# Weights spread over partitions through DRAM, V transposed by DMA, another beginning: one change to a four-layer attention kernel

## The chip, the cores and the metric

The program runs on one core of one Trainium2 chip. The metric is the device time of one execution in microseconds (us). Engines: PE (TensorE), ACT (ScalarE), DVE (VectorE), POOL (GpSimd) and SP (SyncE, which here only issues DMAs); PE's weight loads are listed apart as PEld.

## The reference

x has 2048 rows of 1024 values; there are 32 heads of width 32. Two kinds of layer alternate, each behind a layer norm and each added to x:

```python
def _A_ref(x, wqkv, w_phi, wo):                 # linear attention
    q, k, v = split_heads(x @ wqkv)
    pq = einsum("bhsd,hdf->bhsf", q, w_phi);  pk = einsum("bhsd,hdf->bhsf", k, w_phi)
    phi_q = concatenate([softmax(pq), softmax(-pq)], -1)
    phi_k = concatenate([softmax(pk), softmax(-pk)], -1)
    kv = einsum("bhsf,bhsd->bhfd", phi_k, v);  z = einsum("bhsf->bhf", phi_k)
    num = einsum("bhqf,bhfd->bhqd", phi_q, kv)
    den = einsum("bhqf,bhf->bhq", phi_q, z)[..., None] + 1e-6
    return merge_heads(num / den) @ wo

def _B_ref(x, wqkv, wo):                        # softmax attention
    q, k, v = split_heads(x @ wqkv)
    p = softmax(einsum("bhqd,bhkd->bhqk", q, k) * Dh ** -0.5)
    return merge_heads(einsum("bhqk,bhkd->bhqd", p, v)) @ wo

x = A_x
for _ in range(2):
    x = x + _A_ref(_layernorm(x), A_wqkv, A_w_phi, A_wo)
    x = x + _B_ref(_layernorm(x), B_wqkv, B_wo)
```

## The kernel before, in words

**Layout.** x lies transposed in SBUF for the whole run (`xT`: 1024 features as 8 tiles of 128 partitions, 2048 rows as four *chunks* of 512). A projection of one 128-feature tile for one chunk is eight groups of four matmuls: `mm` splits each 128-wide weight tile into four of 32 columns (rows of the profile with `128*32 128x512`, L529; four such run beside each other on four parts of the array). PSUM has eight banks of 128x512.

**Order.** Nothing is issued where it stands in the source. Each instruction is handed to a list scheduler (`op`, `dma`) with an engine, a planned duration, its dependences, its buffers and a due time (`prio`); the scheduler simulates the engines and buffers and so fixes one order for every engine beforehand. On the chip each engine, and each DMA-issuing queue (SP, ACT and POOL have one each), goes through its list strictly in order and waits where an input isn't there. The tables at the head of the file (`COUNT`, `KP`, `VQ`, `OUT`, ...) are due times and choices for this planner.

**Layer A.** Keys first: features of K, then `kv` and `z` sums over all rows. Then queries, chunk by chunk (c = 0..3), each in two halves of 16 heads (hf = 0, 1), by `a_queries`: four projected 128x512 tiles; ACT takes exp(+) and exp(-) of each; matmuls with `rep` (L938) sum them per head; ACT takes Ln of both sums, DVE subtracts (L948), ACT takes Exp: a *weight* for every head and row, 4 heads in 4 rows of each of four 32-row bands. To multiply it in, it has to be spread over the 32 partitions of its head. `split_hl` (DVE: L891, L892) splits the f32 weight into two bf16 parts, `spread` (PE, L907, stationary operand `selb`) copies it over partitions into PSUM banks, and DVE multiplies exp(-) by it (L955, four per half). Numerators (L970) and denominators (L985) follow; the denominator's reciprocal (ACT: Ln, Exp) is spread in the same way, but *turned* by a band for each tile (`selr`), and DVE multiplies the numerators by it (L996). `a_out` projects the result, and DVE adds it to `xT` (L1009). Then the next layer norm of that chunk starts.

**Layer B.** For each query chunk and each of eight groups of four heads: score matmuls (L1231), exponentials, matmuls with V and with ones (L1279). Most exponentials are ACT's (L1247, on 1536 or 1024 columns at a time); `COUNT` says, for each of 32 (chunk, group) pairs, how many pairs of 512-column units are left to DVE, which computes them by integer arithmetic (`pair`: L1158 twice, L1167, L1170, L1172, L1175, L1177). The sums' reciprocals are written to DRAM (`rd`, L1336) and read back over 32 partitions each (L1338), for DVE's multiplication at L1344. K, Q and V for later groups, weights of layer A and so on are fitted between as *fill* (buffer class "fil"). Keys go to their place by DMAs (L1025), swapped queries by L1046/L1047. PE also issues matmuls without use (`idle`) when it would fall idle. V is computed with the chunk's rows stationary, 256 columns at a time (`b_v`; evacuated by ACT at L1032 or by DVE at L1033).

**Beginning.** Chunk 0 of x is brought in by eight transposing DMAs (L561), SP's and ACT's queue by turns. Layer A's K weights are folded with w_phi (`fold_phi`): their first half is loaded by POOL's queue, their second by SP's (L711), then PE transposes them (L724). Later weights come as slabs (L684, L687). `phi_t` is a constant tile that DVE clears.

Of the kernel before, what the change touches and what calls it, by code (L numbers as in the profile page):

```python
# [12 lines left out]
ALU = mybir.AluOpType  # L13
# [36 lines left out]
LAT = {"PE": 0.2, "ACT": 0.19, "DVE": 0.06, "POOL": 0.2, "SP": 2.0, "AQ": 2.0, "GQ": 2.5}  # L50
# [5 lines left out]
TIE = 9  # L56
# [13 lines left out]
class Sched:  # L70
# [99 lines left out]
    def run(self):  # L170
# [32 lines left out]
        while left:  # L203
# [108 lines left out]
SBUF_ARENA = 172 * 1024 - 256  # L312
# [3 lines left out]
LONG = {"kT", "v", "slab", "slabk", "xn", "xn1", "kvacc", "kvm", "zm", "wnat"}  # L316
MODEST = {"slabk", "xn1", "e1", "vp1", "pkf", "lnw1", "w2o"}
NUMS = 2
LATER = ((33.8, 20.9, 28.9, 13.4), (31.9, 22.9, 4.6, -2.5))
VQ = (((0, 7.0), (45.5, 3.6), (55.2, 7.3)), ((10.4, 7.5), (84.2, 12.8), (150.7, 10.1)))  # L320
FULL = 5
OUT = (37.1, 25.3)
EARLY = (4.0, 0.0)
DUE = 0.0
BOOST = 30.0
EVAC = 20.0
QA = (101.9, 4.8)
# [4 lines left out]
         "rs": 8, "pkf": 1, "cden": 2, "part": 8, "w2r": 1,  # L332
# [8 lines left out]
HOST = ((), (16,), (11, 17), (5, 11, 22), (5, 10, 18, 24))  # L341
# [3 lines left out]
SLABD = (1, 5)  # L345
TOK = (0.0, 0.6, 0.61, 0.62)
SLOW = 6.0
HALF = 4
KGAP = (6.2, 2.4)
LATE = 15.8  # L350
KP = (0, 40.9, 68.0, 103.5, 68.1, 148.3, 180.6, 204.5)
BO = 225
OP0 = (233.8, 267.8, 288.4)
OGAP = (2.5, 2.1, 1.7)
COUNT = ((0, 0, 0, 2, 4, 4, 4, 3, 4, 3, 4, 4, 4, 4, 4, 3, 4, 2, 3, 4, 3, 2, 1, 2, 0, 2, 4, 2, 1, 2, 3, 4),
    (2, 4, 4, 4, 4, 4, 3, 4, 4, 4, 4, 4, 4, 4, 4, 4, 4, 4, 4, 4, 4, 4, 5, 4, 4, 2, 4, 4, 4, 3, 4, 2))
PAIRS = ((), ((0, 2),), ((0, 2), (1, 2)), ((0, 1), (0, 5), (1, 3)), ((0, 1), (0, 5), (1, 1), (1, 5)),
    ((0, 1), (0, 3), (0, 6), (1, 1), (1, 5)), ((0, 1), (0, 3), (0, 6), (1, 1), (1, 3), (1, 6)))
AK = ((0, 201.9), (1, 232.4), (2, 258.8))
OUT1 = ((171.2, 2.7), (179.5, 1.3), (245.9, 1.0))  # L360
# [14 lines left out]
def kernel(  # L375
# [52 lines left out]
    phi_t = const.tile([P, G * P], BF16, tag="phi")  # L428
    nc.vector.memset(phi_t[:].bitcast(U32), 0)
# [24 lines left out]
    for a in range(4):  # L454
        for j in range(4):
            c = (j + a) % 4
            nc.vector.tensor_copy(
                out=selr[32 * a:32 * a + 32, 32 * c:32 * c + 32], in_=selb[32 * a:32 * a + 32, 32 * j:32 * j + 32])
# [16 lines left out]
    gone = []  # L475
    qd = dram_p.tile([P, 2 * G * C512], BF16, tag="qd")
# [78 lines left out]
    def load_x():  # L555
        for lo, hi, prio, us, kb in ((0, 1, -24.0, 1.3, 128), (1, 2, -9.0, 1.3, 400), (2, NC, -8.0, 2.0, 800)):
            last = []
            for po in range(PO):
                q = "AQ" if not lo and po % 2 else "SP"
                last.append(dma(  # L560
                    prio, lambda lo=lo, hi=hi, po=po, q=q: ENG[q].dma_start_transpose(  # L561
                        out=xT[:, po, lo * C512:hi * C512], in_=A_x[0, lo * C512:hi * C512, po * P:(po + 1) * P]),
                    q=q, issue=us, kb=kb))
                if not lo:
                    last[-1].slack = 1.2
            for c in range(lo, hi):
                xdone[c] = last
# [134 lines left out]
    def phi():  # L702
        return phi_t[:].rearrange("p (g n) -> p g n", g=G)

    def fold_phi(col, wd_v, prio, use_pe):
        w_t = []
        if use_pe:
            nb, nv = sb("wnat", PO, D)
            ld = []
            for h, q, at in ((0, "GQ", -23.0), (1, "SP", -20.0)):  # L710
                ld.append([dma(at, lambda h=h, i=i, q=q: ENG[q].dma_start(  # L711
                    out=nv()[:, 2 * i:2 * i + 2, C512 * h:C512 * h + C512],
                    in_=A_w[:, 2 * i:2 * i + 2, col + C512 * h:col + C512 * h + C512]),
                    (), [nb], q=q, kb=256, issue=0.7) for i in range(4)])
                for o in ld[-1]:
                    o.slack = 1.2
# [25 lines left out]
        for fc in range(2):  # L742
# [3 lines left out]
            for m in range(PO):  # L746
                pb, pv = ps("wt", ANY)

                def fn(m=m, pv=pv, fc=fc):
                    for k in range(4):  # L750
# [3 lines left out]
                       [pb] + [w_t[4 * fc + k][0] for k in range(4)], pa, mode="c")  # L754
# [157 lines left out]

# [652 lines left out]
```

## Time and profile before

| | |
|---|---|
| time, median of 3 runs | 2269.91 us (2265.57 to 2270.1) |
| the profiled execution | 2261.7 us; its span 2259.7 us |
| granted PE clock | 1.00 |
| busy: PE, ACT, DVE, POOL | 2170.3, 1987.8, 1844.7, 197.2 us |
| first layer A ("A1") | 0 to 337.0 us |
| first layer B ("B1") | 337.0 to 1222.3 us |
| second layer A ("A2") | 1222.3 to 1424.9 us |
| second layer B ("B2") | 1424.9 to 2248.6 us, then 11.1 us of output |

The borders are the first and the last start of an L1247 exponential in each layer B. A phase of layer A includes the layer norm and the first projections for the layer B behind it. PE's busy time in the phases of layer B includes the matmuls without use, so there a high share does not say that PE is the bound.

### The profile page before, as it was taken

The page shows a single profiled execution, that of the slowest core. Times are in us where ns is not written, and L with a number is a line of the kernel's source. Part 1 is how long each engine was busy: PE and PEld are TensorE (multiplying, and loading weights), DVE is VectorE, ACT ScalarE, POOL GpSimd, SP SyncE. Part 2 cuts the span into 40 slices and gives each one's busy share as a digit, 9 for nine tenths or more (in the row PEclk, how much of TensorE's full clock was granted, in tenths as well). Part 3 has the DMA queues.
Part 4 walks back from the last instruction along what each step waited for, and adds up shares of the span by engine and source line. Part 5 has one row for each costly group of instructions (what it writes and reads, how often), then busy time and mean ns, then how long its engine had stood idle before and what let it go on. Part 6 is the DMA issues. An engine that isn't in the chain of part 4 may idle for free.

```text
span 2259.7 us, 82520 instructions
## 1 busy us (share of the span) xinstructions
PE 2170.3 (96%) x36752; PEld 869.3 (38%) x36752; DVE 1844.7 (82%) x2754; ACT 1987.8 (88%) x1939; POOL 197.2 (9%) x301
## 2 busy tenths in 40 slices
PE   5999999999999999999999999999999999999999
PEld 3554454344333333333333444433333333333333
DVE  6887772498899779678788788799899999997986
ACT  4435759999999999999998555899999999999998
POOL 1020000000001010121224100000000000100000
PEclk9999999999999999999999999999999999999999
DMA  8320011111123231222235101111111101201111
GB/s 180 68 67 23 9 42 40 45 33 26 45 62 108 63 82 40 68 82 82 82 109 152 40 5 30 33 28 34 39 32 28 40 19 26 72 24 42 47 35 38
DMA packets 123085, 119.67 MB, mean 53 GB/s; under 512 B 59944, under 2 KB 100968, under 8 KB 122728
## 3 DMA queue, kind: packets, MB, share of 16 engines
q1 hardware_dynamic: 102392, 56.64, 9.8%
q0 software_dynamic: 17584, 56.70, 8.8%
q8 instruction: 287, 4.70, 0.9%
q10 hardware_dynamic: 2752, 1.05, 0.2%
q14 instruction: 70, 0.57, 0.1%
HBM read 78.71 MB, written 14.14 MB: 41 GB/s over the span
## 4 chain that ended last, share of the span: by engine, by line
PE 29%; ACT 20%; DVE 10%; issue 6%; DMA 1%; POOL 0%; SPq 0%; ACTq 0%; DVEq 0%; POOLq 0%
ACT arena L1247 19%; PE psum L529 15%; PE psum L1279 6%; PE psum L1231 6%; DVE arena L1177 1%; DVE arena L1158 1%; DVE arena L1175 1%; DVE arena L1170 1%; DVE arena L1167 1%; DVE arena L1344 1%; DVE arena L1172 1%; ACT arena L799 1%; DMA arena<-arena 1%; DVE arena L1033 0%; DVE arena L1295 0%
## 5 line engine op out<-in xcount | busy, mean ns | idle before, releaser
L1247 ACT ACTIVATE arena<-psum 128x1536 bf16<-128x1536 f32 (+1 forms) x1366 | 1671.2, 1432 | 10.7 <-PE psum L1231 6.0
L529 PE MATMUL psum<-arena 128*32 128x512 bf16 (+1 forms) x18432 | 1055.2, 357 | 15.4 <-issue 3.9
L529 PEld LDWEIGHTS <-arena 128*32 128x32 bf16 x18944 | 461.1, 96 | 445.3 <-issue 171.7
L1279 PE MATMUL psum<-arena 128*32 128x512 bf16 x4096 | 624.4, 383 | 4.5 <-DVE arena L1295 3.5
L1279 PE MATMUL psum<-arena,ones_bf 128*32 128x512 bf16 x4096 | 624.1, 383 | 1.3 <-issue 1.3
L1231 PE MATMUL psum<-arena 32*128 32x512 bf16 x4096 | 537.1, 383 | 32.9 <-ACT arena L1247 25.9
L1231 PEld LDWEIGHTS <-arena 32*128 32x128 bf16 x4096 | 157.3, 91 | 561.3 <-issue 554.6
L1158 DVE TENSOR_SCALAR arena<-psum 128x512 int32<-128x512 f32 x414 | 280.8, 684 | 102.8 <-PE psum L1231 96.4
L1177 DVE SCALAR_TENSOR_TENSOR arena<-arena 128x1024 int16<-128x1024 int32 x207 | 251.5, 1216 | 4.2 <-PE psum L1279 0.2
L1279 PEld LDWEIGHTS <-arena 128*32 128x32 bf16 x4096 | 163.5, 95 | 225.4 <-issue 174.7
L1279 PEld LDWEIGHTS <-ones_bf 128*32 128x32 bf16 x4096 | 161.2, 95 | 25.3 <-issue 10.2
L1167 DVE TENSOR_SCALAR arena<-arena 128x1024 f16<-128x1024 int16 x207 | 141.2, 686 | 5.3 <-DMA arena<-arena 1.6
L1170 DVE TENSOR_TENSOR arena<-arena 128x1024 f16<-128x1024 f16 x207 | 140.7, 683 | 5.3 <-DMA arena<-arena 0.6
L1175 DVE TENSOR_TENSOR arena<-arena 128x1024 f16<-128x1024 f16 x207 | 140.8, 683 | 3.4
L684 POOL DMA_DIRECT2D arena<-in_B_wqkv_dram x46 | 42.1, 915 | 1095.4 <-PE psum L529 320.9
L1033 DVE CAST arena<-psum 128x512 bf16<-128x512 f32 x128 | 87.4, 683 | 59.6 <-PE psum L529 59.4
L799 ACT ACTIVATE arena<-psum 128x512 bf16<-128x512 f32 x80 | 43.1, 596 | 83.5 <-PE psum L529 60.6
L803 DVE TENSOR_REDUCE arena<-arena 128x32 f32<-128x1024 bf16 x64 | 77.2, 1213 | 36.8 <-ACT arena L799 36.6
L529 PE MATMUL psum<-xT,onesD 128*32 128x512 bf16 x1112 | 99.5, 381 | 1.1 <-DVE arena L1033 0.5
L1295 DVE COPY arena<-psum 128x512 f32<-128x512 f32 x126 | 86.1, 683 | 14.2 <-PE psum L1279 13.9
L812 DVE TENSOR_TENSOR arena<-psum,arena 128x1024 bf16<-128x1024 f32 x64 | 77.5, 1218 | 13.3 <-PE psum L529 9.8
L1172 DVE TENSOR_SCALAR arena<-arena 128x1024 f16<-128x1024 f16 x207 | 86.4, 421 | 1.9
(120 smaller groups left out, 1378.9 us busy)
## 6 DMA issues: line engine op xcount, KB each, us to landing
arena<-rd SPq DMA_DIRECT2D x62, 256.0 KB
arena<-in_B_wqkv_dram POOLq DMA_DIRECT2D x58, 256.0 KB, 4.2
arena<-in_B_wo_dram POOLq DMA_DIRECT2D x40, 256.0 KB, 4.0
arena<-in_A_wqkv_dram POOLq DMA_DIRECT2D x36, 256.0 KB, 4.8
arena<-arena SPq DMA_DIRECT2D x256, 32.0 KB
arena<-wd_k POOLq DMA_DIRECT2D x32, 256.0 KB, 4.7
arena<-arena SPq DMA_DIRECT2D x96, 64.0 KB
arena<-arena SPq DMA_DIRECT2D x248, 2.0 KB
```

Source lines behind the costliest of these rows:

```text
L529: nc.tensor.matmul(out_[ks, :], lhsT=lhsT[:, ks], rhs=rhs, start=start, stop=stop, tile_position=(0, 32 * k), skip_group_check=True)
L1033: return op("DVE", dve_us(512), lambda: nc.vector.tensor_copy(out=dst(), in_=src()), [dep], bufs, prio)
L1158: o = op("DVE", dve_us(512), lambda: nc.vector.tensor_scalar(out=x_v()[:, k, :].bitcast(I32), in0=s_v()[:, x * C512:(x + 1) * C512], scala ...
L1167: last = op("DVE", 1024 / 1920 + 0.15, lambda: nc.vector.tensor_scalar(out=z(), in0=x_v().bitcast(I16).rearrange("p a (n two) -> p a n two ...
L1170: last = op("DVE", 1024 / 1920 + 0.15, lambda: nc.vector.tensor_tensor(out=u(), in0=z(), in1=z(), op=ALU.mult), [last], [z_b, u_b], prio + ...
L1172: last = op("DVE", 1024 / 3840 + 0.15, lambda: nc.vector.tensor_scalar(out=u(), in0=u(), scalar1=POW2_C[0], scalar2=POW2_C[1], op0=ALU.mul ...
L1175: last = op("DVE", 1024 / 1920 + 0.15, lambda: nc.vector.tensor_tensor(out=u(), in0=z(), in1=u(), op=ALU.mult), [last], [z_b, u_b], prio + ...
L1177: return op("DVE", dve_us(1024), lambda: nc.vector.scalar_tensor_tensor(out=y_v().bitcast(I16), in0=x_v().bitcast(I32), scalar=128.0 / BIT ...
L1231: nc.tensor.matmul(out=s_v()[:, x * C512:(x + 1) * C512], lhsT=kT[g][1]()[r, pp, d * P:(d + 1) * P], rhs=q_of[(qc, g)][1]()[r, (pp + j // ...
L1247: ex = op("ACT", act_us(w * C512), lambda s_v=s_v, e_v=e_v, w=w: nc.scalar.activation(out=e_v(), in_=s_v()[:, 0:w * C512], func=ACT.Exp, s ...
L1279: nc.tensor.matmul(out=a_v()[col:col + 32, :], lhsT=v_v()[:, kc % 4, o:o + DH] if what == 0 else ones_bf[:], rhs=ev()[:, x * C512:(x + 1) ...
L1295: cp = op("DVE", dve_us(512), lambda t_v=t_v, a_v=a_v: nc.vector.tensor_copy(out=t_v(), in_=a_v()), [last], [a_b, t_b], prio - 4)
```

## The change

**1. Two of four chunks through DRAM** (`WIRE`: chunks 1 and 2 of each layer A, weights and reciprocals). A new `carry` takes the place of `split_hl` and `spread` there: on SP's queue four writes of 4x512 f32 to DRAM (tile `wd`, L943), and then reads that repeat each DRAM row over 32 partitions (L954): for weights four reads of four rows, for reciprocals seven, since the turn cuts them in 4, 3+1, 2+2 and 1+3 rows. DVE then multiplies from SBUF instead of PSUM (L1007, formerly L955; L1052, formerly L996). The weights' multiplications get an earlier due time (`pre`), and each half of each chunk its own (`EAR`).

**2. V of head groups 0 and 1 turned** (`b_vt`): the weights are stationary and the chunk's rows move, 512 wide; ACT (group 0, in layer A's phase) or DVE (group 1, in layer B) evacuates V transposed, and four transposing DMAs of 128x128 on SP's queue (L1161) turn it.

**3. Beginning.** Four transposing DMAs for chunk 0's first four feature tiles, all on SP; the other four tiles are loaded as they lie by two 256 KB DMAs on POOL's queue (L564), transposed by 16 matmuls on PE (L584) and copied by DVE (L590). The first half of the K weights is one 1 MB DMA on ACT's queue (L735).

**4. Two buffers less**: the constant `phi_t` becomes a tile of the arena, and `pair` computes in `y` where it had a tile `u`. The arena grows by 2 KB.

**5. The planner's tables**, most of them. `COUNT` adds up to 88 instead of 86 pairs for DVE in B1 and to 125 instead of 121 in B2. The instructions of L1247 of 1536 columns become 506 and 432 (from 510 and 440), those of 1024 columns 177 and 251 (from 173 and 243).

```diff
+    def carry(r_b, r_v, dep, prio, turn):
+        at_d = wd_v[len(sent)]
+        sent.append(prio)
+        st = [dma(prio, lambda a=a: nc.sync.dma_start(out=at_d[a], in_=r_v()[32 * a:32 * a + 4, :]),
+                  [dep], [r_b], kb=8) for a in range(4)]
...
+            n = turn * a % 4
+            for lo, hi, to in ((0, 4 - n, n), (4 - n, 4, 0)):
+                if hi > lo:
+                    o = dma(prio, lambda a=a, v=v, lo=lo, hi=hi, to=to: nc.sync.dma_start(
+                        out=v()[32 * to:32 * (to + hi - lo), :],
+                        in_=at_d[a, lo:hi].unsqueeze(1).to_broadcast([hi - lo, 32, C512])), [st[a]], [b], kb=150 * (hi - lo))
...
-        h_b, h_v, h = split_hl(lm_b, lm_v, w, pre)
-        for a, (b_, v_, bm) in enumerate(spread(h_b, h_v, h, prio, selb)):
+        if c in WIRE[layer][0]:
+            wide_ = carry(lm_b, lm_v, w, pre, 0)
+        else:
+            h_b, h_v, h = split_hl(lm_b, lm_v, w, pre)
+            wide_ = spread(h_b, h_v, h, prio, selb)
...
+        if c in WIRE[layer][1]:
+            wide_ = carry(r_b, r_v, l4, prio, 1)
...
+    def b_vt(g, c, prio, w, vT, banks, eng):
+        wb, ww, wd = w
+        xb, xv, fin = xnB[c]
+        pb, pv = ps("fil", banks)
+        h = g % 4
+        m = mmg2(pb, pv, lambda po: ww()[:, po, h * P:h * P + P], lambda po: xv()[:, po, :], fin, wd, [xb, wb], prio)
+        a_b, a_v = sb("kt", C512)
+        cp = evac(eng, a_v, pv, m, [pb, a_b], prio)
+        v_b, v_v, done = vT[(g // 4, c)]
+        for t in range(TB):
+            done[(t, h)] = dma(prio, lambda t=t: nc.sync.dma_start_transpose(
+                out=v_v()[:, t, h * P:h * P + P], in_=a_v()[:, t * P:t * P + P]), [cp], [a_b, v_b], kb=32, issue=VT[0])
...
-            for t in range(TB):
-                b_v(0, c, t, pr + 43 + LATER[layer][c] + 0.1 * t, bv_s[0], vT, ANY, "ACT", 0, 256)
+            b_vt(0, c, pr + 43 + LATER[layer][c], bv_s[0], vT, ANY, "ACT")
...
+        for c in range(NC):
+            b_vt(1, c, at + VE[layer][0] + VE[layer][1] * c, bv_s[0], vT, FIL, "DVE")
```

**SP's queue at the beginning.** `xT<-in_A_x_dram` is a transposing load of x, `in_A_wqkv_dram` are layer A's weights. Before:

```order
L561 DMA_TRANSPOSE xT<-in_A_x_dram 128x512 x4
L711 DMA arena<-in_A_wqkv_dram 128x2x512 x4
L561 DMA_TRANSPOSE xT<-in_A_x_dram 128x512 x5
L687 DMA arena<-in_A_wqkv_dram 128x2x512 x8
L764 DMA wd_k<-arena 128x8x512
```

And now:

```order
L572 DMA_TRANSPOSE xT<-in_A_x_dram 128x512 x4
L738 DMA arena<-in_A_wqkv_dram 128x2x512 x4
L572 DMA_TRANSPOSE xT<-in_A_x_dram 128x512 x7
L715 DMA arena<-in_A_wqkv_dram 128x2x512 x8
L791 DMA wd_k<-arena 128x8x512
```

SP's own list hardly differs; what went is ACT's four transposes of the same tiles, which stood behind its table load, and ACT's queue now starts the 1 MB of weights instead.

**SP's queue in the first layer A, behind the loads of layer B's weights.** Before (L1046, L1047: swapped queries; L1025: keys of layer B):

```order
L684 DMA arena<-in_B_wqkv_dram 128x8x128 x2
L687 DMA arena<-in_B_wqkv_dram 128x2x512 x4
L1046 DMA arena<-arena 64x512
L1047 DMA arena<-arena 64x512
L1025 DMA arena<-arena 64x256 x20
```

And now, where L943 writes weights or reciprocals and L954 reads them back spread:

```order
L715 DMA arena<-in_B_wqkv_dram 128x2x512 x4
L943 DMA wd__120<-arena 4x512 x4
L954 DMA arena<-wd__120 128x1x512 x4
L943 DMA wd__120<-arena 4x512 x4
L954 DMA arena<-wd__120 128x1x512 x4
L943 DMA wd__120<-arena 4x512 x4
L954 DMA arena<-wd__120 128x1x512
L954 DMA arena<-wd__120 96x1x512
L954 DMA arena<-wd__120 32x1x512
L954 DMA arena<-wd__120 64x1x512 x2
L954 DMA arena<-wd__120 32x1x512
L954 DMA arena<-wd__120 96x1x512
```

The three carries shown are chunk 1's weights for both halves and its first half's reciprocals. Five more follow on the same queue; the first transfers for layer B (L1102, L1103, formerly L1046, L1047) now stand inside the sixth (chunk 2's weights, second half).

**DVE's list around chunk 1.** L948 (now L996) subtracts the logarithms, L955 (now L1007) multiplies weights in, L996 (now L1052) reciprocals, L1009 (now L1065) adds a projected tile to x. Before:

```order
L948 TENSOR_TENSOR arena<-arena 128x512
L996 TENSOR_TENSOR arena<-arena,psum 128x512 x4
L891 CAST arena<-arena 128x512
L892 SCALAR_TENSOR_TENSOR arena<-arena,hl 128x512
L1009 TENSOR_TENSOR xT<-xT,psum 128x512
L955 TENSOR_TENSOR arena<-arena,psum 128x512 x4
L1009 TENSOR_TENSOR xT<-xT,psum 128x512 x2
```

And now:

```order
L996 TENSOR_TENSOR arena<-arena 128x512
L1065 TENSOR_TENSOR xT<-xT,psum 128x512 x2
L1007 TENSOR_TENSOR arena<-arena 128x512
L1065 TENSOR_TENSOR xT<-xT,psum 128x512
L1007 TENSOR_TENSOR arena<-arena 128x512
L1065 TENSOR_TENSOR xT<-xT,psum 128x512
L1007 TENSOR_TENSOR arena<-arena 128x512 x2
L1065 TENSOR_TENSOR xT<-xT,psum 128x512 x2
```

The multiplications, which stood together behind a split, now stand one by one between the additions of chunk 0's output, in the order in which the reads were issued.

More of the change, by code (lines that the diff above doesn't have):

```diff
@@ L47, in __init__ @@
         self.slack = 0.0
-LAT = {"PE": 0.2, "ACT": 0.19, "DVE": 0.06, "POOL": 0.2, "SP": 2.0, "AQ": 2.0, "GQ": 2.5}
+LAT = {"PE": 0.2, "ACT": 0.21, "DVE": 0.06, "POOL": 0.2, "SP": 2.0, "AQ": 2.0, "GQ": 2.5}
 SWITCH = 0.1
@@ L55 @@
 RING = 0.5
-TIE = 9
+TIE = 7
 LOOK = 8
@@ L454 @@
     for a in range(4):
[L455 to L458, printed above, removed]
+        rows = slice(32 * a, 32 * a + 32)
+        nc.vector.tensor_copy(out=selr[rows, 32 * a:P], in_=selb[rows, 0:P - 32 * a])
+        if a:
+            nc.vector.tensor_copy(out=selr[rows, 0:32 * a], in_=selb[rows, P - 32 * a:P])
     nc.vector.tensor_tensor(out=pick[:, 0:1], in0=fold[:, 0:1], in1=fold[:, 4:5], op=ALU.add)
@@ L1353 @@
     load_x()
+    phi_b, phi = sb("phi", G, P)
+    phi_0 = op("DVE", 0.5, lambda: nc.vector.memset(arena[:, phi_b.at // 2:phi_b.at // 2 + G * P].bitcast(U32), 0),
+               (), [phi_b], -30.0)
     phi_ld = [dma(-18.0, lambda j=j: nc.gpsimd.dma_start(
         out=phi()[32 * j:32 * j + 32, :, 32 * j:32 * j + 32],
-        in_=A_w_phi.rearrange("(g j) i f -> j i g f", j=4)[j]), (), (), q="GQ", kb=16) for j in range(4)]
+        in_=A_w_phi.rearrange("(g j) i f -> j i g f", j=4)[j]), [phi_0], [phi_b], q="GQ", kb=16) for j in range(4)]
     store = {}
@@ L1521 @@
                     for i in range(4)]
+                for o in xnA[c]:
+                    o.slack = 3.0
     def idle():
```

143 lines of the change are left out of this document (92 added, 51 removed), and 1 row of the table QUOTA.

## The prediction

> **What bounds the kernel now.** I read the page's first part, then busy time by stage (windows at the borders of the layers), then the groups by line inside a stage.
>
> ```profile
> PE 2170.3 (96%) x36752; PEld 869.3 (38%) x36752; DVE 1844.7 (82%) x2754; ACT 1987.8 (88%) x1939; POOL 197.2 (9%) x301
> core 0: us, PE busy (x) PEld busy (x) DVE busy (x) ACT busy (x) POOL busy (x), PEclk, DMA share, GB/s
> 0.00:50.00 50.00, 25.33 (x538) 15.46 (x542) 29.05 (x66) 21.73 (x30) 6.66 (x16) 1.00 0.79 180
> 0.00:337.00 337.00, 306.29 (x6831) 164.66 (x6835) 262.87 (x374) 172.26 (x291) 32.57 (x68) 1.00 0.29 65
> 337.00:1222.30 885.30, 858.82 (x13637) 314.05 (x13625) 689.27 (x1022) 877.98 (x746) 122.64 (x172) 1.00 0.24 68
> 1222.30:1424.90 202.60, 199.01 (x3951) 95.93 (x3955) 158.38 (x224) 116.80 (x207) 17.38 (x32) 1.00 0.12 35
> 1424.90:2248.60 823.70, 799.48 (x12213) 290.90 (x12202) 729.70 (x1127) 818.41 (x692) 24.58 (x29) 1.00 0.13 35
> L529 PE MATMUL psum<-arena 128*32 128x512 bf16 x4032 | 231.3, 379 | 1.6 <-issue 1.6
> L529 PE MATMUL psum<-arena 128*32 128x512 bf16 x2776 | 162.2, 380 | 3.0 <-DVE arena L1318 1.3 <-issue 1.1 <-DMA arena<-in_B_wo_dram 0.3
> ```
>
> Rows three to seven are the first 50 us, A1, B1, A2 and B2. PE's 96% is an average over two regimes. In the A phases PE bounds: it is idle for 3.6 of 202.6 us in A2, and of A1's 30.7 us of idle time 24.7 lie in the first 50. In the B phases ACT bounds: idle for 7.3 and 5.3 us. PE's high share there includes matmuls without use, so PE work saved in B is worth nothing by itself. The last two rows (PE by line, 50:337 and A2) give the price of a 512-wide matmul in an A phase: 231.3/4032 = 57 ns, 162.2/2776 = 58 ns. A change within 0.2% (4.5 us) counts as the same, about what a measurement of this kernel can tell from none.
>
> **Part by part.** *The beginning.*
>
> ```profile
> 0.75 13.90 SPq L561 DMA_TRANSPOSE xT<-in_A_x_dram  x4
> 10.80 9.19 ACTq L561 DMA_TRANSPOSE xT<-in_A_x_dram  x4
> 13.55 0.59 PE L581 MATMUL psum<-xT,onesD 128*32 128x512 bf16 x1 [9.44 <-DMA xT<-in_A_x_dram]
> 21.59 0.58 PE L581 MATMUL psum<-xT,onesD 128*32 128x512 bf16 x1 [6.62 <-DMA xT<-in_A_x_dram]
> ```
>
> The timeline shows SP's and ACT's transposes one after another: ACT's first goes out at 10.80, and PE's mean over features stops 9.44 and 6.62 us for them. Without ACT's four, SP's four can follow each other, and the other half of x comes by plain loads. PE should get the last of x at about 14 us instead of 21.59: −7.5. It could be −11 if the loads come at once, and only −3 if the 1 MB of weights on ACT's queue, started at the same time, takes the DMA engines from them (they are already 0.79 busy in the first 50 us). The new transposes cost PE 16 matmuls, between 58 ns each (a 512-wide one of four side by side, above) and 273 ns (the mean of a 256-wide one, below): 0.9 to 4.4 us; I take 1.4 and set it against A1. SP's list passes nothing new here, and `phi` only changes its place.
>
> *V turned and spreads gone, on PE in the A phases.*
>
> ```profile
> L529 PE MATMUL psum<-arena 128*32 128x256 bf16 x320 | 10.5, 273 | 0.0
> L907 PE MATMUL psum<-arena,selr 32*128 32x512 bf16 x32 | 4.1, 384 | 0.0
> L907 PE MATMUL psum<-arena,selb 32*128 32x512 bf16 x32 | 3.9, 383 | 0.0
> L529 PE MATMUL psum<-arena 128*32 128x256 bf16 x320 | 10.2, 273 | 0.0
> L907 PE MATMUL psum<-arena,selb 32*128 32x512 bf16 x32 | 4.4, 383 | 0.0
> L907 PE MATMUL psum<-arena,selr 32*128 32x512 bf16 x32 | 4.1, 384 | 0.0
> L892 DVE SCALAR_TENSOR_TENSOR arena<-arena,hl 128x512 bf16<-128x512 bf16 x32 | 24.0, 749 | 0.8
> L891 DVE CAST arena<-arena 128x512 bf16<-128x512 f32 x32 | 13.5, 421 | 28.3 <-ACT arena L992 28.3
> ```
>
> (Three rows for A1, three for A2, two of the whole kernel.) A1 loses the 256-wide matmuls (−10.5) and gains 128 of 512 columns at 57 ns (+7.3): −3.2. In A2 64 of the 128 new ones stand ahead of the first score in the order, 64 × 58 ns = 3.7: −10.2 + 3.7 = −6.5. Half of the spreads go: −4.0 in A1, −4.3 in A2. With the 1.4 us above A1 gives −5.8, A2 −10.8. DVE loses 16 pairs of L891/L892, 16 × 1.17 = 18.7 us, but waits for PE in these phases: nothing. The 16 transposes per group of V on SP's queue stand behind the last carry and are needed only by layer B's matmuls; I cost them at nothing, covered by the start of B. If that cover fails, they cost at most what four transposes of four times the size took at the start, 13.90 us per layer.
>
> *Layer B, on ACT and DVE.*
>
> ```profile
> L1247 ACT ACTIVATE arena<-psum 128x1536 bf16<-128x1536 f32 x440 | 614.5, 1570 | 2.1 <-PE psum L1231 1.5 <-PE psum L1279 0.6
> L1247 ACT ACTIVATE arena<-psum 128x1024 bf16<-128x1024 f32 x243 | 249.0, 1159 | 1.8 <-PE psum L1231 1.6
> L1032 ACT CAST arena<-psum 128x256 bf16<-128x256 f32 x7 | 2.6, 384 | 1.2 <-PE psum L529 1.2
> L1158 DVE TENSOR_SCALAR arena<-psum 128x512 int32<-128x512 f32 x414 | 280.8, 684 | 102.8 <-PE psum L1231 96.4
> L1177 DVE SCALAR_TENSOR_TENSOR arena<-arena 128x1024 int16<-128x1024 int32 x207 | 251.5, 1216 | 4.2 <-PE psum L1279 0.2
> L1167 DVE TENSOR_SCALAR arena<-arena 128x1024 f16<-128x1024 int16 x207 | 141.2, 686 | 5.3 <-DMA arena<-arena 1.6
> L1170 DVE TENSOR_TENSOR arena<-arena 128x1024 f16<-128x1024 f16 x207 | 140.7, 683 | 5.3 <-DMA arena<-arena 0.6
> L1175 DVE TENSOR_TENSOR arena<-arena 128x1024 f16<-128x1024 f16 x207 | 140.8, 683 | 3.4
> L1172 DVE TENSOR_SCALAR arena<-arena 128x1024 f16<-128x1024 f16 x207 | 86.4, 421 | 1.9
> ```
>
> One ACT instruction narrowed from 1536 to 1024 columns saves 614.5/440 − 249.0/243 = 1.397 − 1.025 = 0.37 us. Four in B1, eight in B2: −4.5. Fewer evacuations of V on ACT (seven of 0.37 in B2, about as many in B1, against one or two of twice the width): about −4. Six pairs more go to DVE at (280.8+251.5+141.2+140.7+140.8+86.4)/207 = 5.03 us: B2's DVE goes from 729.7 by 4 × 5.03 + 4 evacuations of 0.68 to about 753 of 820 us, which leaves it behind ACT in total but not everywhere. Of −8.5 I keep −5; 0 and −9 are the ends. `u` in the place of `y` costs no operation, as long as a pair doesn't wait for the one before.
>
> Without the carries' waits: −7.5 − 5.8 − 10.8 − 5 = −29, a profiled time of 2261.7 − 29 = 2232.7. The median of the runs lies 2269.91 − 2261.7 = 8.2 above the profiled run; with that, 2241.
>
> *The carries.* Before has one operation of their kind, L1338: 256 KB read from DRAM, four rows over 32 partitions each.
>
> ```profile
> 16.00:18.00 2.00, 0.00 (x0) 0.00 (x0) 0.00 (x0) 0.00 (x0) 0.00 (x0) 1.00 0.90 273
> 492.76 0.59 SPq L1338 DMA_DIRECT2D arena<-rd  x1
> 494.10:496.80 2.70, 2.70 (x61) 1.40 (x58) 2.67 (x5) 2.70 (x3) 0.00 (x0) 1.00 0.28 97
> 726.18 0.60 SPq L1338 DMA_DIRECT2D arena<-rd  x1
> 731.17 0.69 DVE L1344 TENSOR_TENSOR arena<-arena 128x512 bf16<-128x512 f32 x1 [0.42 <-DMA arena<-rd]
> 777.82 0.59 SPq L1338 DMA_DIRECT2D arena<-rd  x1
> 786.01 0.69 DVE L1344 TENSOR_TENSOR arena<-arena 128x512 bf16<-128x512 f32 x1 [1.72 <-DMA arena<-rd]
> 2234.09 0.33 SPq L1336 DMA_DIRECT2D rd<-arena  x1
> 2235.62 0.58 SPq L1338 DMA_DIRECT2D arena<-rd  x1
> ```
>
> The read issued at 492.76 moves its data from 494.10 to 496.80: 2.7 us at 97 GB/s with a DMA share of 0.28, while plain loads (16:18) reach 273 GB/s at 0.90. So such a read is held to about a quarter of the 16 engines, four or five, and keeps them for 2.7 us. Issue to use is 4.99 us alone and 8.19 beside other loads; a write has landed 1.53 us after its issue. Every L943 to L954 chain therefore takes at least 1.5 + 5 = 6.5 us, plus its issues (0.33 and 0.59 each).
>
> No row of before has two of these reads in flight, and there lies the open price. If four reads go **side by side** on different engines, a carry takes about 9 us: 4 × 0.33 + 1.5 + 4 × 0.59 + 4. If they go **behind each other** on the same quarter, a weights' carry holds it for 4 × 2.7 = 10.8 us and a reciprocals' for 5 × 2.7 = 13.5 (the reads of 4, 3, 2, 2 and 3 rows counted alike, as reads of before differ in no such way; the two single rows counted at nothing). Rows of before bear on it only by the share of 0.28: a quarter in use is the same quarter or not. I take behind each other, since the share shows that the engines are chosen by the shape and the shape is the same every time, and it is the more careful end. [...]
>
> What covers them: chunk 1's carries start with its sums (`rep`), and the last carry has to be through before PE's output projection of chunk 2. By the order of after, PE has between these points 150 groups of eight 512-wide matmuls, 1200 × 57 ns = 68 us, and about 10 us of sums, numerators, denominators and chunk 3's spreads: 78 us. Eight carries behind each other are 4 × 10.8 + 4 × 13.5 = 97 us of reads. To that come the first write and Ln/Exp (taken at 4 us) and turnarounds, since a reciprocal's carry can't be written before its own weights are multiplied in: at 1.5 + 1.3 us for five to seven of them, 14 to 20 us. 115 to 121 against 78: 37 to 43 late. PE can still slip some of chunk 3 ahead; I take **35 us per layer, 70 in all**. Side by side, a chain of weights, numerators, denominators, reciprocals is 25 us (two carries at 9, and 7 taken for what lies between) against 38 us of PE rows from chunk 1's sums to its own output projection (76 groups of the 150, and less than half of the rest): nothing. What stands behind the wait: DVE's list has L1007/L1052 between additions to x (L1065), so a late read also holds PE's PSUM banks; SP's queue holds layer B's keys behind the last carries.
>
> **The rivals.** *(0) Forecast: behind each other.* 2261.7 − 29 + 70 = 2302.7, with 8.2 about **2310**. With lateness of 25 to 45 us per layer and the bounds of the other terms, 2285 to 2336. Chance 0.53, of that 0.06 beyond the upper end (reads beside weight loads: 8.19 instead of 4.99 us).
>
> *(1) Side by side, all hidden: faster.* For it: nothing shows the same quarter, and PE is only late if a chain exceeds 38 us. 2261.7 − 29 + 8.2 = **2241**, with B's and the start's ends 2232 to 2252. Chance 0.36. It decides at a carry of about 17 us: below it, a carry hides.
>
> *(2) Partly late*: behind each other, but two of four overlapped, or PE's list has more to put ahead. 5 to 20 us per layer, 2251 to 2281, likeliest 2262. Chance 0.11: half of it faster, 0.04 the same, the rest slower.
>
> *(3) The change does not do what it says at the start.* The slabs behind it set the end of the start:
>
> ```profile
> 28.78 5.68 SPq L687 DMA_DIRECT2D arena<-in_A_wqkv_dram  x8
> ```
>
> These eight loads stand behind x's on SP in both orders. If PE waits for them as before, the start's −7.5 shrinks to −3; that moves each case by 4.5 us and lies inside the ranges.
>
> **How the numbers follow.** The likeliest case gives 2310. The range must reach to (1), so 2236 to 2332: below lies some of (1), above some of (0), together under 0.2. Faster: 0.36 + 0.05 = 0.41; same 0.04; slower 0.53 + 0.02 = 0.55. Both signs carry weight: given (0), 2285 to 2332.
>
> **What would show it.** In the first layer A of after: L954's reads landing 2.7 us apart at a DMA share near 0.28 (forecast), or together at a share near 1 (rival 1); PE's idle time in A1 and A2 behind `DVE arena L1007` and `L1052`, about 35 us each, or under 5; PE's last stop for x at 14 us; L1247's counts as in the order and ACT's idle time in B2 under 8 us. The forecast is wrong if the A phases are shorter than before, or if PE waits in B for V or for DVE.

## The result, and the profile after

The changed kernel takes 2351.32 us (median of 4 runs, 2348.48 to 2356.97) against 2270.01 of before: a ratio of 1.037 (95% interval 1.0345 to 1.0393). It is slower, as forecast, but by 81 us where 40 were forecast, and 2351 lies above the range's end of 2332. The profiled execution took 2356.97 us, its span is 2355.1, 95.4 longer than before's.

Busy time by stage of after (the first 50 us, A1, B1, A2, B2, and A1's last 174 us), with the granted clock in the third column from the end:

```profile
0.00:50.00 50.00, 35.40 (x848) 22.04 (x851) 37.16 (x68) 24.02 (x35) 6.21 (x17) 1.00 1.06 216
0.00:374.40 374.40, 319.72 (x6630) 167.08 (x6634) 257.96 (x352) 172.34 (x286) 31.50 (x66) 0.94 0.34 83
374.40:1273.30 898.90, 860.47 (x13552) 311.62 (x13545) 702.25 (x1042) 874.62 (x740) 125.36 (x170) 1.00 0.24 68
1273.30:1516.00 242.70, 208.91 (x3688) 96.52 (x3691) 151.06 (x205) 118.02 (x203) 19.59 (x36) 0.92 0.22 68
1516.00:2343.60 827.60, 800.40 (x12102) 285.25 (x12097) 745.68 (x1159) 814.32 (x685) 25.08 (x28) 1.00 0.14 36
200.00:374.40 174.40, 139.28 (x2228) 61.70 (x2224) 96.15 (x131) 74.39 (x122) 6.38 (x8) 0.88 0.22 68
```

In before, 1222.3 and 2248.6 are the ends of the last exponentials of B1 and B2; they start at 1221.2 and 2247.4. By starts, as in after, before's phases are 337.0, 884.2, 203.7 and 822.5 us, and these figures are used from here on. A1 is 37.4 us longer, B1 14.7, A2 39.0, B2 5.1. Both A phases lose although PE has fewer instructions there, and they lose in two ways: PE is idle (54.7 of 374.4 us in A1, 33.8 of 242.7 in A2), and it is also *busier* than before (319.7 against 306.3 us in A1, 208.9 against 200.1 in A2) with fewer matmuls, at a granted clock of 0.94 and 0.92; 0.88 in A1's stretch of the carries.

The beginning went as forecast, and better. Timeline of PE in after:

```profile
8.53 0.60 PE L584 MATMUL psum<-ident,arena 128*128 128x128 bf16 x4 [8.53 <-DMA arena<-in_A_x_dram]
11.00 1.46 PE L584 MATMUL psum<-ident,arena 128*128 128x128 bf16 x12 [1.86 <-DMA arena<-in_A_x_dram]
```

From 11.00 on PE has all of chunk 0, where it waited until 21.59 before: the end that the prediction gave as the best case.

The carries on SP's queue in A1 (timeline of after), two windows over the data of the second line's and the sixth line's reads, and DVE's multiplications by what the first two carries brought:

```profile
199.94 1.31 SPq L943 DMA_DIRECT2D wd__120<-arena  x4
201.42 3.13 SPq L954 DMA_DIRECT2D arena<-wd__120  x4
204.76 2.27 SPq L943 DMA_DIRECT2D wd__120<-arena  x4
214.53 2.53 SPq L954 DMA_DIRECT2D arena<-wd__120  x4
217.84 2.00 SPq L943 DMA_DIRECT2D wd__120<-arena  x4
228.49 4.95 SPq L954 DMA_DIRECT2D arena<-wd__120  x7
233.49 3.30 SPq L943 DMA_DIRECT2D wd__120<-arena  x4
244.40 4.79 SPq L954 DMA_DIRECT2D arena<-wd__120  x7
```

```profile
202.90:214.00 11.10, 10.53 (x204) 4.61 (x193) 5.89 (x9) 2.05 (x4) 0.00 (x0) 1.00 0.27 99
229.90:244.00 14.10, 9.05 (x134) 3.76 (x127) 5.79 (x7) 7.06 (x14) 0.00 (x0) 0.86 0.23 79
```

```profile
209.02 0.69 DVE L1007 TENSOR_TENSOR arena<-arena 128x512 bf16<-128x512 bf16 x1 [0.37 <-DMA arena<-wd__120]
211.64 0.69 DVE L1007 TENSOR_TENSOR arena<-arena 128x512 bf16<-128x512 bf16 x1 [1.26 <-DMA arena<-wd__120]
214.24 0.69 DVE L1007 TENSOR_TENSOR arena<-arena 128x512 bf16<-128x512 bf16 x1 [1.92 <-DMA arena<-wd__120]
219.86 0.69 DVE L1007 TENSOR_TENSOR arena<-arena 128x512 bf16<-128x512 bf16 x1 [0.96 <-DMA arena<-wd__120]
222.44 0.69 DVE L1007 TENSOR_TENSOR arena<-arena 128x512 bf16<-128x512 bf16 x1 [1.15 <-DMA arena<-wd__120]
```

Four reads issued within 3.1 us move their 1 MB in 11.1 us, at a share of 0.27; their users start 2.6 us apart. Four reads in flight take about what four of before's single reads take one after the other (4 × 2.7 = 10.8 us). Seven reads of a turned carry, also 1 MB in all, take 14.1 us. And a second thing shows that the prediction had only as a turnaround: the next carry's *writes*, issued at 204.76, land only when the reads ahead of them are through, so that its reads go out at 214.53, ten us later.

Who waited in A1's last 174 us of after (six of the rows; engine, line, releaser, us in total, times, longest):

```profile
DVE arena L1052 <- DMA arena<-wd__120: 33.3, 16, 7.7
DVE arena L1007 <- DMA arena<-wd__120: 19.4, 12, 2.4
PE psum L536 <- DVE arena L1052: 15.9, 7, 6.6
ACT arena L975 <- DMA wd__120<-arena: 12.5, 2, 6.7
ACT arena L1030 <- DMA wd__120<-arena: 8.0, 1, 8.0
PE psum L986 <- ACT arena L975: 6.4, 1, 6.4
```

DVE waits 52.7 us for the reads; behind it PE waits for DVE. The fourth and fifth row are the writes again: a buffer that a write still has to read isn't free for ACT, and PE then waits for ACT.

### The profile page after: what moved, and what is told of

Read it like the earlier page. It is cut to its first block, busy times and chain, and to the rows that moved or that the text cites. A ratio compares the mean times of both kernels' runs of the same rounds, so it can differ in the third digit from the quotient of the medians.

```text
span 2355.1 us, 81643 instructions
## 1 busy us (share of the span) xinstructions
PE 2196.9 (93%) x36116; PEld 866.1 (37%) x36116; DVE 1861.9 (79%) x2765; ACT 1982.8 (84%) x1915; POOL 201.5 (9%) x299
## 4 chain that ended last, share of the span: by engine, by line
PE 33%; ACT 18%; DVE 14%; DMA 6%; issue 6%; SPq 1%; POOL 0%; DVEq 0%; ACTq 0%; POOLq 0%
ACT arena L1319 16%; PE psum L536 15%; PE psum L1351 9%; PE psum L1303 8%; DMA arena<-wd__120 3%; DVE arena L1230 3%; DVE arena L1249 2%; DVE arena L1239 2%; DVE arena L1242 1%; DMA arena<-arena 1%; DVE arena L1247 1%; DVE arena L1416 1%; DVE arena L1089 1%; DVE arena L1244 1%; ACT arena L826 1%
## 5 line engine op out<-in xcount | busy, mean ns | idle before, releaser
L1319 ACT ACTIVATE arena<-psum 128x1536 bf16<-128x1536 f32 (+1 forms) x1366 | 1667.6, 1401 | 34.0 <-PE psum L1303 15.1
L536 PE MATMUL psum<-arena 128*32 128x512 bf16 (+2 forms) x18432 | 1094.3, 365 | 57.5 <-DVE arena L1052 25.5
L1351 PE MATMUL psum<-arena 128*32 128x512 bf16 x4096 | 629.7, 385 | 14.6 <-DVE arena L1367 6.4
L1351 PE MATMUL psum<-arena,ones_bf 128*32 128x512 bf16 x4096 | 629.8, 385 | 0.0
L1230 DVE TENSOR_SCALAR arena<-psum 128x512 int32<-128x512 f32 x426 | 290.9, 686 | 81.2 <-PE psum L1303 71.6
L1249 DVE SCALAR_TENSOR_TENSOR arena<-arena 128x1024 int16<-128x1024 int32 x213 | 259.3, 1217 | 1.9
L1351 PEld LDWEIGHTS <-arena 128*32 128x32 bf16 x4096 | 162.8, 95 | 231.6 <-issue 179.3
L1351 PEld LDWEIGHTS <-ones_bf 128*32 128x32 bf16 x4096 | 160.3, 95 | 32.8 <-issue 18.9
L1089 DVE CAST arena<-psum 128x512 bf16<-128x512 f32 x136 | 93.2, 685 | 74.4 <-PE psum L536 66.4
L1242 DVE TENSOR_TENSOR arena<-arena 128x1024 f16<-128x1024 f16 x213 | 145.7, 684 | 7.8 <-PE psum L1351 1.3
L1239 DVE TENSOR_SCALAR arena<-arena 128x1024 f16<-128x1024 int16 x213 | 146.1, 686 | 4.0 <-PE psum L1351 0.2
L1247 DVE TENSOR_TENSOR arena<-arena 128x1024 f16<-128x1024 f16 x213 | 145.6, 683 | 3.0
L1030 ACT COPY arena<-psum 128x512 f32<-128x512 f32 x64 | 35.4, 592 | 95.5 <-PE psum L1022 66.1
L826 ACT ACTIVATE arena<-psum 128x512 bf16<-128x512 f32 x80 | 43.1, 597 | 83.7 <-PE psum L536 74.8
L1367 DVE COPY arena<-psum 128x512 f32<-128x512 f32 x126 | 86.3, 685 | 19.7 <-PE psum L1351 14.1
L975 ACT ACTIVATE arena<-psum 128x512 bf16<-128x512 f32 x128 | 70.4, 615 | 31.8 <-DMA wd__120<-arena 17.8
```

What stands on the lines that cost most here:

```text
L536: nc.tensor.matmul(out_[ks, :], lhsT=lhsT[:, ks], rhs=rhs, start=start, stop=stop, tile_position=(0, 32 * k), skip_group_check=True)
L1089: return op("DVE", dve_us(512), lambda: nc.vector.tensor_copy(out=dst(), in_=src()), [dep], bufs, prio)
L1230: o = op("DVE", dve_us(512), lambda: nc.vector.tensor_scalar(out=x_v()[:, k, :].bitcast(I32), in0=s_v()[:, x * C512:(x + 1) * C512], scala ...
L1239: last = op("DVE", 1024 / 1920 + 0.15, lambda: nc.vector.tensor_scalar(out=z(), in0=x_v().bitcast(I16).rearrange("p a (n two) -> p a n two ...
L1242: last = op("DVE", 1024 / 1920 + 0.15, lambda: nc.vector.tensor_tensor(out=u(), in0=z(), in1=z(), op=ALU.mult), [last], [z_b, u_b], prio + ...
L1247: last = op("DVE", 1024 / 1920 + 0.15, lambda: nc.vector.tensor_tensor(out=u(), in0=z(), in1=u(), op=ALU.mult), [last], [z_b, u_b], prio + ...
```

## The experiments

Theory: the reads queue behind each other on one quarter of the DMA engines (the share is 0.27; which engines they use no row shows), and the A phases are late by that. Rivals: the order itself, the planner's tables, or V's transposes.

In what follows a unit is 512 columns of L1319's exponentials; "the 100th unit" and "the stretch" are the start of the instruction that holds it in the first layer B, and the time from the first such start to it. A1, B1 and so on end at such starts.

**No chunk carried.**

```diff
-WIRE = (((1, 2), (1, 2)), ((1, 2), (1, 2)))
+WIRE = (((), ()), ((), ()))
```

> The changed kernel with no chunk carried through DRAM (all four spread by PE as before), everything else as changed; the planner makes its order anew. Theory (the carries' reads queue on one quarter of the DMA engines, and this alone makes layer A late): A1 about 325 us and A2 about 197 instead of 374.4 and 242.7, granted clock 1.00 there, 2245 to 2260 in all. Rival (the lateness lies in the new order and tables, or in V's transposes, and not in the carries): A1 and A2 stay over 350 and 220, 2310 or more.

2276.72 us, ratio 1.0050 (1.0033 to 1.0067). A1 ends at 323.2 and PE's waits for DVE's two multiplications are gone there: this points at the carries, though the order is a new one. A2 is 205.7 us, 37 less than in after, but not the 197 expected. The total stays above before's instead of 2245 to 2260, and the stretch at layer B's start is 64.7 us against 47.8 in before. So what the rest of the change should have brought is missing too, and not in A1.

**The same carries over more engines.** All lists stay the same, only shapes differ: each row is written four times, and a read takes 16 rows over 8 partitions each.

```diff
...
-in_=r_v()[32 * a:32 * a + 4, :]),
+in_=r_v()[32 * a:32 * a + 4, :].unsqueeze(1).to_broadcast([4, 4, C512])),
...
-in_=at_d[a, lo:hi].unsqueeze(1).to_broadcast([hi - lo, 32, C512])), [st[a]], [b], kb=150 * (hi - lo))
+in_=at_d[a, lo:hi].rearrange("j r n -> (j r) n").unsqueeze(1).to_broadcast([4 * (hi - lo), 8, C512])), [st[a]], [b], kb=150 * (hi - lo))
```

> The same carries at the same places of every engine's list, but each row is written four times (16 rows of DRAM for 4) and a read takes 16 rows over 8 partitions each instead of 4 over 32. Theory: the reads spread over about four times as many engines, four land in about 4 us instead of 11.2, the waits for the multiplications go; A1 about 322 us, A2 about 194, clock 1.00, 2235 to 2260 in all. Rival (what makes it late is the order itself: multiplications between additions in DVE's list, eight carries in one SP list, whatever a read takes): A1 and A2 change by less than 10 us, 2335 or more.

2266.84 us, ratio 1.0000 (0.9989 to 1.0012): 84.5 us less than the changed kernel, with every list in the same order. The first four reads now move their data from 203 to about 208 us, 5 us instead of 11.1, at a share of 0.73 instead of 0.27 (last row): 2.7 times, where about four times as many engines were expected. By stage (the first row is A1, then B1, A2, B2, A1 from 200 on, and the reads):

```profile
0.00:325.90 325.90, 301.02 (x6634) 158.30 (x6638) 255.87 (x352) 171.07 (x286) 31.50 (x66) 1.00 0.41 97
325.90:1223.30 897.40, 861.45 (x13542) 311.50 (x13538) 702.16 (x1042) 874.84 (x739) 125.55 (x170) 0.99 0.24 68
1223.30:1422.90 199.60, 191.77 (x3702) 98.25 (x3694) 149.12 (x205) 116.61 (x203) 19.54 (x36) 1.00 0.30 87
1422.90:2249.50 826.60, 799.71 (x12102) 285.02 (x12097) 745.54 (x1159) 814.31 (x686) 25.08 (x28) 1.00 0.14 36
200.00:325.90 125.90, 120.40 (x2200) 56.02 (x2196) 93.24 (x128) 71.79 (x120) 6.39 (x8) 1.00 0.37 100
203.00:208.00 5.00, 5.00 (x100) 2.35 (x100) 3.09 (x5) 0.05 (x1) 0.00 (x0) 1.00 0.73 225
```

A1 is 48.5 us shorter than in after, A2 43.1. Since the rows are the same, the split needs no model, but for records that a trace may lack (the two spans differ by 94.2 us, the medians by 84.5): in A1 18.7 us of PE's busy time (319.72 − 301.02) and 29.8 of idle time, in A2 17.1 and 26.0. The price of a matmul shows it again (PE by line, after from 200 to 374.4, then this run from 200 to 325.9):

```profile
L536 PE MATMUL psum<-arena 128*32 128x512 bf16 x1808 | 120.0, 413 | 17.3 <-DVE arena L1052 15.9 <-ACT arena L1088 1.4
```

```profile
L536 PE MATMUL psum<-arena 128*32 128x512 bf16 x1780 | 104.3, 381 | 0.2 <-DVE arena L1052 0.2
```

The same matmul costs 66 ns instead of 59 (busy time by count) where the clock is granted at 0.88. The rival on the order falls. What stays open: B1 is as long as in after, 13 us longer than before.

**The reads on POOL's queue**, unchanged in shape.

```diff
-lambda a=a, v=v, lo=lo, hi=hi, to=to: nc.sync.dma_start(
+lambda a=a, v=v, lo=lo, hi=hi, to=to: nc.gpsimd.dma_start(
```

> The changed kernel's reads of four rows, unchanged in shape, issued on POOL's queue instead of SP's, writes still on SP's; lists otherwise the same. [...] If the shape alone fixes the engines, or a read of this shape is slow on any queue, four still take about 11 us and the time stays at 2340 to 2360.

2274.84 us (one run), far below the 2340 to 2360 expected if the four reads still took about 11 us; A1 is 336.8 us and A2 205.2. The first 4 us of the first four reads, and the whole of them:

```profile
206.20:210.20 4.00, 4.00 (x80) 2.01 (x76) 2.02 (x4) 0.63 (x1) 1.32 (x2) 1.00 0.66 136
206.20:213.70 7.50, 7.26 (x136) 3.20 (x132) 4.57 (x9) 1.28 (x3) 1.58 (x3) 1.00 0.57 147
```

At 136 GB/s the first row holds only half of the four reads' 1 MB; all four take about 7.5 us at a share of 0.57, against 11.1 at 0.27, with the same DRAM rows and shapes. So neither the shape nor the repeated reading of a row explains the 11.1 us by itself: on POOL's queue the same reads have twice the share. Which engines a read uses on either queue no row shows, and what holds the four at 7.5 us is open.

**Weights alone carried**, reciprocals spread by PE.

```diff
+WIRE = (((1, 2), ()), ((1, 2), ()))
```

> The changed kernel with only the weights of chunks 1 and 2 carried, their reciprocals spread by PE; new order by the planner. Theory: four carries of 11 us per layer, 45 us, are covered by the PE rows of 78 us that follow; A1 about 325 to 335, A2 about 198 to 208, 2250 to 2275 in all. Rival (each carry costs its share, about 6 us, wherever it stands): half of the loss stays, A1 about 350, A2 about 220, 2300 in all.

2298.15 us (one run), at the rival's figure and not at the theory's; A1 is 339.9 us, A2 214.8. Half of the carries, 31 us above the run with sixteen rows, though in another order. Two groups of PE's from 200 to 340 us (by line; L1022 are numerators, L1037 denominators):

```profile
L1022 PE MATMUL psum<-arena 32*32 32x512 bf16 x192 | 9.4, 380 | 5.2 <-DVE arena L1007 5.2
L1037 PE MATMUL psum<-arena 128*32 128x512 bf16 x48 | 4.5, 386 | 2.4 <-DVE arena L1007 2.1 <-DVE xT L1065 0.2
```

The idea that a carry is free while a later total of PE rows covers it doesn't hold: PE's list has the same half's numerators soon behind, and there PE waits, 7.3 us for the weights. The rest of the 31 us was not traced.

**V as before**, with the sixteen-row carries: the two `b_vt` calls taken back to `b_v`.

> The sixteen-row carries with V of both head groups computed as in the kernel before, so without the 128x128 DMA transposes; the planner makes the order anew. There, with V transposed, the first layer B reached its 100th unit of 512 exponential columns at 385.4 us though layer A ended at 325.9; the kernel before needed 47.8 us for this stretch, that one 59.5. Theory: the transposes, 1.26 us each on SP's queue ahead of layer B's keys, take back the gain at layer B's start; without them A1 is about 329 us, the stretch about 48, the 100th unit at 375 to 379, and the total 2260 to 2270, since PE and ACT get V's former work back (about 10 us in all). Rival (layer B's start waits for something else, weights or PE): the 100th unit stays at 383 or later, 2270 or more in all.

2255.17 us, ratio 0.9947 (0.9932 to 0.9962). The 100th unit is there at 375.6, 48.3 us after the first: the theory's case, and the total is even below it. A2 is 211.5 us, 12 more than with V by DMA; how much of that is the former V and how much the new order was not settled.

**Keys ahead of V's transposes.** Sixteen-row carries, V by DMA:

```diff
-VT = (0.6, 1.0)
-VE = ((-14.0, 3.3), (-9.4, 14.0))
+VT = (1.26, 1.0)
+VE = ((5.0, 4.0), (-9.4, 14.0))
...
-            done[(t, h)] = dma(prio, lambda t=t: nc.sync.dma_start_transpose(
+            done[(t, h)] = dma(prio + 15.0, lambda t=t: nc.sync.dma_start_transpose(
```

> The sixteen-row carries and V transposed by DMA, but the transposes get a due time 15 later, V of head group 1 in the first layer B is due 19 later, and the planner counts 1.26 us for a transpose's issue, so that fewer of them stand ahead of layer B's keys. Theory (transposes ahead of the keys cost layer B's start): 100th unit at 374 to 381 us, 2253 to 2263 in all. Rival (something else): 385, 2265 or more.

**2244.99 us, ratio 0.9904 (0.9889 to 0.9919): 1.0% less than before, clear of the noise.** The 100th unit at 373.9, a stretch of 50.0 us. SP's queue in the run with sixteen rows only, and in this one (L1081 are layer B's keys):

```profile
324.71 15.13 SPq L1161 DMA_TRANSPOSE arena<-arena  x12
339.94 3.12 SPq L1081 DMA_DIRECT2D arena<-arena  x4
344.67 15.72 SPq L1161 DMA_TRANSPOSE arena<-arena  x12
360.50 2.88 SPq L1081 DMA_DIRECT2D arena<-arena  x4
```

```profile
320.11 2.44 SPq L1081 DMA_DIRECT2D arena<-arena  x4
322.92 7.09 SPq L1161 DMA_TRANSPOSE arena<-arena  x5
335.66 2.41 SPq L1081 DMA_DIRECT2D arena<-arena  x4
```

Twelve transposes held the queue for 15.1 us ahead of four keys. But the keys are not what the sixteen-row run stood for: between its first exponential and the 100th unit the profile has no engine waiting for L1081. ACT and PE stood for the transposes themselves (ACT's timeline, then two of L1161's waiters; L1351 multiplies with V):

```profile
337.86 1.45 ACT L1319 ACTIVATE arena<-psum 128x1536 bf16<-128x1536 f32 x1 [5.06 <-DMA arena<-arena]
```

```profile
  ACT arena L1319: 5.1, 1
  PE psum L1351: 2.6, 2
```

An exponential doesn't read V. It reads PSUM and writes to the arena, so it most likely waited for a place there that a transpose still had to read. In the run with the keys ahead, no engine waits for L1161 in this stretch. Since three lines changed at once and the order is new, these runs don't say which line did it.

**The same with the narrow reads**, so the changed kernel with only the transposes' three lines.

> The changed kernel with its reads as they were (four rows over 32 partitions), and only the transposes' due times and price moved, as in the run that put fewer of them ahead of layer B's keys. Theory (the two losses are separate: late carries in the A phases, late keys at layer B's start): A1 stays at 370 to 378 us and A2 at 238 to 246, the stretch from the first exponential to the 100th unit of layer B falls from 59 to about 50, 2330 to 2345 in all. Rival (the transposes on SP's queue also delay the carries): A1 and A2 get shorter by over 8 us each, 2325 or less.

2335.11 us (one run), A1 369.7, A2 243.1, the stretch 50.0: the two losses are separate, but for 4.7 us in A1.

**The beginning alone**: before's tables, spreads and V, with the new beginning and two buffers less.

> Before with the new beginning and the two buffers less alone: its own tables, its spreads by PE, its V. Theory: x is there 10 us earlier and nothing takes that back; A1 about 327 us, the 100th unit at about 375, 2254 to 2261 in all. Rival (the slabs that follow, or layer B's weights, hold it): A1 over 333, 2264 or more.

2274.74 us, ratio 1.0039 (1.0027 to 1.0052). A miss in the total: A1 ends at 327.0 and the 600th unit of B1 comes at 600.8 against 612.3, so the gain is there; then the new order gives 11 us back between the 600th and the 1200th unit and A2 is 11 us longer. Why stays open.

**The beginning and sixteen-row carries** with before's tables:

> The same as the run with the beginning alone, but with the sixteen-row carries for chunks 1 and 2. Theory: half of the spreads' PE time, 4 us per layer A, comes on top and no read is waited for: 2244 to 2256 in all, faster than both kernels. Rival (carries cost what they save, by SP's queue ahead of layer B's keys): no better than the beginning alone, 2256 to 2264.

2295.75 us, ratio 1.0135 (1.0113 to 1.0158): a miss. A1 ends at 342.9, 16 us later than without the carries; the cause stays open.

**The planner's price of a read.** Cheaper, dearer (both on the fastest kernel, where 150 KB per row stood), and, for the narrow reads with the transposes moved, near what the chip takes (the ends of the changed line):

```diff
+kb=60 * (hi - lo))
...
+kb=200 * (hi - lo))
...
+kb=1120 if hi - lo > 1 else 100)
```

> The fastest so far (sixteen-row carries, keys ahead of transposes) with the planner's price for a carry's read cut from 150 to 60 KB per row, so that it puts less work between a read and its use. Theory (the order has room around the carries): a few us less in each A phase, 2236 to 2244. Rival (the planner's dearer reads were a margin that reality needs, or the order is only different): 2245 to 2260.

> The fastest so far (sixteen-row carries, keys ahead of transposes) with the planner's price for a read raised from 150 to 200 KB per row. Theory (each new order differs by some tens of us from luck, not from the price): anywhere from 2245 to 2285. Rival (a dearer price is a margin that pays): 2238 to 2246.

> The changed kernel's own reads (four rows over 32 partitions, and so on), the transposes' due times moved as before, and the planner told what such a read takes behind others: 2.8 us of the ring for each read of more than one row instead of 0.4 per row (1.5 for four). Theory (the loss in the A phases is the difference between the planner's price and the chip's): with the true price it puts other work ahead of the multiplications; waits fall to under half, A1 335 to 350 us, A2 210 to 225, 2265 to 2300 in all. Rival (there is no work left to put there, the chain of eight carries is longer than what can stand beside it): A1 over 360, A2 over 235, 2320 or more.

2288.24 us (ratio 1.0092, 1.0071 to 1.0114), 2262.45 (0.9982, 0.9973 to 0.9992) and 2365.29 (one run). Neither the dearer nor the cheaper price paid here. Two other orders of the same work lie 17 and 43 us above the best, so the total of a single new order can't tell what an edit costs; among the runs above only the one with sixteen rows keeps every list. With the true price the narrow reads stay late, A1 372.1 and A2 266.0: in none of the three orders with eight such carries are they covered.

## Why the prediction was right or wrong

**The sign, and the carries' reads behind each other,** were right: four reads take 11.1 us against 4 × 2.7 = 10.8 foreseen, a turned carry's reads 14.1 against 13.5. That it is "the same quarter" was the author's estimate from the share of 0.28; no run shows which engines a read uses. What the runs show is that the shape counts (0.27 for four rows over 32 partitions each, 0.73 for sixteen over 8, both on SP's queue), but not alone, as the prediction took it: on POOL's queue the four rows reach 0.57. The turned carry, with the same bytes cut in 4, 3+1, 2+2 and 1+3 rows, takes 14.1/11.1 = 1.27 times as long as the one cut in fours. Nor were POOL's reads wholly side by side: by an estimate from 2.7 us for one and the 2.8 us in which the four were issued, they would be done in 5.5 us, and 7.5 were measured. Rival 1 falls.

**The size: the term of the carries.** Forecast 70, measured 84.5 (after against the same lists with sixteen rows; 81.2 with each set against before's runs beside it). By layer that is 48.5 and 43.1 in the profiles, where 35 was taken and 45 was the upper bound. The idle time was *over*estimated: 29.8 and 26.0 us, 56 instead of 70. What was not in the sum at all is the clock: in after, with PE's waits, it is 0.94 in A1 and 0.92 in A2 against 1.00 with sixteen rows, and the same matmuls take 18.7 and 17.1 us more, 36 in all. The rows were multiplied by 57 ns as if that were a constant.

**The size: the −29.** This failed more: with the carries mended the kernel stands at 2266.84, no gain, where 2241 was forecast. Of the 41 us between the 40 forecast and the 81 measured, 29 lie here and the rest in the carries. The step that failed is "The 16 transposes per group of V ... I cost them at nothing, covered by the start of B". They aren't covered: in the sixteen-row run ACT stands 5.1 us and PE 2.6 us for them in B1's start (PE waiting in B for V is one of the signs of a wrong forecast that the prediction names), and the first 100 units take 59.5 us instead of 47.8, in B2 53.4 instead of 50.4. Without the transposes B1's take 48.3, with them due later 50.0. The bound of 13.9 us per layer came near B1's 11.7 by luck. The row that it was read from spans a gap in the queue (its four transposes last 1.1 to 1.3 us each, and the fourth starts only at 13.52), and it let the cost go with the size, while 24 transposes of a quarter of the size held SP's queue for 15.1 + 15.7 us. The other terms of the −29 in the sixteen-row run, by starts: A1 −11.1 (−13.3 forecast), A2 −4.1 (−10.8). The run with the keys ahead gets 20.9 of the 29 (2265.86 − 2244.99), some of which may be a lucky order.

The terms one by one, in the profile of that run (span 17.1 us shorter than before's): the beginning and A1 forecast at −13.3 together, measured 323.8 − 337.0 = −13.2. A2 forecast at −10.8, measured 198.0 − 203.7 = −5.7, with small waits of PE left, such as 1.6 us behind L1390 and 1.3 behind L1088. Layer B at −5: B2 819.8 against 822.5, B1 889.2 against 884.2, a loss of 2.3 in sum. ACT's busy time falls in both (876.9 to 875.5, 817.2 to 813.0), but its idle time in B1 grows by more; why was not settled.

**Covers by sums.** Setting 78 us of PE rows against the whole chain was the wrong comparison, as the weights alone suggest: a wait is decided between each carry and its own first use. The rival at the start (later slabs hold it) fell.

## What to carry to other kernels

Before a transfer replaces engine work, look at the share of the DMA engines and the rate that its like reaches on its queue (here 0.27 and 99 GB/s for four rows over 32 partitions each, 0.73 and 225 for sixteen over 8), at what is issued behind it on the same queue, and at who needs the place that it reads from: writes, frees of buffers, the next layer's first inputs. Ask for each wait what stands between the issue and its *own* first use; a total over the phase hides it. And where PE will wait for some us at a time, as in after's A1, price its other work at a lower clock too: there a matmul cost 66 ns at 0.88 instead of 59 at 1.00.

## What the runs showed of the hardware that was not expected

A granted clock of 0.88 over 174 us in which PE was busy for 80%, against 1.00 with the same list and nearly no waits (PE idle for 5.5 of 125.9 us). The 0.88 is a mean: in after's records the clock is whole or half (three windows of after, then the stops of PE that end just before the first and within the third):

```profile
215.80:219.20 3.40, 3.40 (x36) 1.53 (x32) 0.69 (x1) 2.90 (x4) 0.00 (x0) 0.50 0.27 89
219.30:229.40 10.10, 6.92 (x127) 3.07 (x123) 3.46 (x5) 2.60 (x3) 0.00 (x0) 1.00 0.21 78
243.20:249.90 6.70, 4.24 (x41) 1.81 (x44) 4.71 (x6) 4.89 (x10) 0.00 (x0) 0.50 0.19 65
```

```profile
214.99 0.39 PE L1022 MATMUL psum<-arena 32*32 32x512 bf16 x4 [1.56 <-DVE arena L1007]
245.66 0.59 PE L986 MATMUL psum<-arena,rep 128*32 128x512 bf16 x1 [6.41 <-ACT arena L975]
```

All eight half stretches of A1 behind 200 us begin during a stop of PE of 1.5 us or more, or within 1 us of its end, and last 3.4 to 10.2 us. In the sixteen-row run the clock is 1.00 over A1. A stop alone doesn't decide it: behind one of 2.30 us, which ended at 114.27 in after, the clock stayed whole. A run that changes PE's stops and nothing else was not made.

And a transposing DMA holds its queue for nearly as long when it moves a quarter of 128x512, 1222 ns against 1302 by the medians (rows by line: of x from DRAM in after, of V within SBUF in the sixteen-row run; min/median/max ns):

```profile
L572 SPq DMA_TRANSPOSE xT<-in_A_x_dram x20: 1130/1302/3381, 0.7 to 45.2; - x20
```

```profile
L1161 SPq DMA_TRANSPOSE arena<-arena x24: 1094/1222/1783, 324.7 to 359.2; - x24
```
